# A ninth key block in 16-bit parts, halved products for a lone block, and re-placed tanh steps in a fused attention and MLP kernel

## The chip, the core and the metric

The kernel runs on one core of a Trainium2 chip. The metric is device time in microseconds for one launch; the table below has the median of three runs. The engines are named as in the profile: PE multiplies matrices (PEld is its weight load), DVE is the vector engine, ACT the scalar engine that evaluates exp and tanh, POOL the general engine, SP the engine that only issues DMAs.

## What is computed

The input `x` has 2048 tokens of 640 numbers. It is normalised once and goes into two branches whose results are added to `x`.

```python
xn = _layernorm(x, axis=-1)
# branch A: 32 heads of 20, softmax over 2048 keys
qkv = (xn @ wqkv) -> q, k, v
p = softmax(q @ k.T * 20 ** -0.5)
A = (p @ v) @ wo
# branch B: per token, 640 -> 1536 -> 640
y = _layernorm(xn, axis=-1)
B = gelu(y @ w1 + b1) @ w2 + b2
return x + A + B
```

All inputs and outputs are 32-bit floats, and the kernel keeps close to that precision: most products are made of two 16-bit parts of each factor, in three passes.

## The kernel before, in words

**Start and projections** (to about 215 us). `x` is normalised, transposed and multiplied by `wqkv` in four chunks of 512 tokens. At the very start PE has nothing to do until the first chunk is normalised; `warm(n)` (L231) fills such places with n multiplications of a constant tile. Between them `add_squares(i)` (L556) adds up the squares of the q weights, each waiting for a sum from ACT. Then four token blocks are transposed (L564 to L568), each after its normalisation on DVE (L270), and `scale_of` (L570) turns the sum of squares into the scale of the q weights. The projections `qkp` (L337) follow.

**Attention with the MLP in its gaps** (about 215 to 1271 us). The work is a list of 256 groups. A group is four blocks of 128 keys for one pair of heads and 512 tokens; four groups, key blocks 0 to 3, 4 to 7, 8 to 11 and 12 to 15, make a run over all keys, and there are 64 runs (16 head pairs, two halves of the tokens, two chunks in each half). For each key block `scores` (L742) makes the scores of two heads on PE (L748) and their exp on ACT (L750) into a 32-bit tile `p`. Three PSUM buffers hold scores.

`SPLIT` (L27) tells how a key block meets the values. For a **split** block `rest` (L757) subtracts on DVE the upper 16 bits of `p` (read as bf16, `upper`) from `p` itself and stores the rest as 16-bit `low` (L762); there are four buffers for `low`. `pv` (L767) then makes four products with the upper bits, two heads times the high and the low part of the values, and two with `low` and the high part of the values alone. For a **whole** block it makes two 32-bit products, one for each head. All of these are recorded at L779, in `product`. A product fills 32 of the 128 output rows: four products that go to the four different sets of 32 rows run side by side on PE, and each set of four is called a round here. With two split and two whole blocks in a group the upper bits take two rounds, the `low` products one, and the 32-bit products one, which PE runs as two matmuls each.

The order is written out by hand (L1191 to L1215). In a group come: the scores of two blocks; `tick()`, which lets each waiting side job emit its next step; the `low` of the first block; a piece of filling work on PE (`other`, L1177, which hands out 1.265 us for each group from a chain of MLP and projection work); the scores of the other two blocks; `tick()`; the `low` of the other blocks; and `pv` of the group **before**. DVE, ACT and PE each take their instructions in the order in which they were emitted.

The filling work is `layer1` (L1005: 30 matmuls `pu` for two of twelve blocks of the hidden layer, 256 tokens) and `layer2` (L1043: 36 matmuls `py`). Six `layer1` calls stand beside four `layer2` calls for the 256 tokens before: after the first and the fourth `layer1` no `layer2` follows, after the others one does (L1068 to L1075). For the first 256 tokens there is no `layer2` at all. All of these use one PSUM buffer, `m`, so the next call's first matmul waits until DVE has read the last one's result: `gelu` (L947) reads `pu` in its first step (L951), `addup` reads `py` (L981). `gelu` goes on in five more steps: two DVE operations on `u` and `w` (L953, L955), one more (L957), tanh on ACT (L961), and three on DVE (L963 to L965). If `reading[0]` is set, the tanh is put off by one `tick`, so that it does not stand in the half group in which ACT reads out the finished attention output (`ev`, L800). There is one buffer for `u` and one for `w`; when a new `gelu` begins, the one that is still active is run to its end first (L1020 to L1024).

**The end** (about 1271 us to the end). `projection` (L1112) makes the last product with `wo` (`z`, L1137) in 256-token pieces. For the tokens of the second half it needs the last heads' result, which `finish` (L861) divides by the softmax sums and writes to `oscr`; a piece reads it back as `ot` (L1087). `finish` waits a fixed number of ticks, `W1` before it adds the sums (L911, L913) and `W2` (L936) before it adds, multiplies and splits the result (L937 to L943).

Of the kernel before, what the change touches and what calls it, by code (L numbers as in the profile page):

```python
# [19 lines left out]
S, D, H, DH, F = 2048, 640, 32, 20, 1536  # L20
KD = D // P
KF = F // P
NKB = S // P
VW = DH + 1
PAD = 32 - VW
VROW = H * VW + PAD
SPLIT = (1, 1, 0, 0) * (NKB // 4)  # L27
NPAIR = H // 2
EPS = 1e-5
TOP = 15.5  # L30
# [14 lines left out]
def mha_mlp_kernel(tc, x, wqkv, wo, w1, b1, w2, b2, out):  # L45
    nc = tc.nc
# [3 lines left out]
    with (  # L50
# [23 lines left out]
        vhalf = vfull.bitcast(F16)  # L74
# [100 lines left out]
        with tc.tile_pool(name="pa", bufs=2) as pa, tc.tile_pool(name="pa1", bufs=1) as pa1, tc.manual_schedule():  # L175
# [55 lines left out]
            def warm(n):  # L231

                ps = psO.tile([P, 512], F32, tag="o", name="warm")
                for _ in range(n):
                    nc.tensor.matmul(ps[:, :P], ones, ones, start=True, stop=True)
# [322 lines left out]
                nc.tensor.matmul(pq[:, :1], ones, accs["q"][:, i : i + 1], start=i == 0, stop=i == KD - 1)  # L558

            add_squares(0)  # L560
            warm(3)
            add_squares(1)
            warm(4)
            for j in range(4):  # L564
                for k in range(KD - 1):
                    nc.tensor.transpose(pt[k][:, j * P : (j + 1) * P], xts[0][j][:, k * P : (k + 1) * P], ident)
# [101 lines left out]
        with ExitStack() as scope:  # L668
# [98 lines left out]
            def pv(units):  # L767

                g, hf, cc, kb0 = units[0][:4]
                if kb0 == 0:
                    pv.o = psO.tile([P, 512], F32, tag="o", name="o")
                    pv.begun = set()
                last = units[-1][3] == NKB - 1

                def product(q, src, v0, t):
                    nc.tensor.matmul(pv.o[32 * q : 32 * q + 32, :], src[:, v0 - PAD * (1 - q % 2) :][:, :32], t,  # L779
                                     start=q not in pv.begun, stop=last, skip_group_check=True)  # L780
                    pv.begun.add(q)

                split = [(u[3], upper(u[4]), u[5]) for u in units if SPLIT[u[3]]]
                whole = [(u[3], u[4]) for u in units if not SPLIT[u[3]]]
                of16 = lambda kb, a: 2 * PAD + kb * 2 * VROW + (2 * g + a) * 2 * VW
                of32 = lambda kb, a: PAD + kb * VROW + (2 * g + a) * VW
                for kb, up, _ in split:
                    for a in range(2):
                        product(2 * a, vhalf, of16(kb, a), up[:, a])
                        product(2 * a + 1, vhalf, of16(kb, a) + VW, up[:, a])  # L790
                for a in range(2):
                    for n, (kb, _, low) in enumerate(split):
                        product(2 * a + n % 2, vhalf, of16(kb, a), low[:, a])
                for a in range(2):
                    for n, (kb, pt) in enumerate(whole):
                        product(2 * a + n % 2, vfull, of32(kb, a), pt[:, a])
                if last:
                    if cc == 0:
                        evs[g, hf] = m1.tile([P, 2, 512], F32, tag="ev", name="ev")
                    nc.scalar.activation(evs[g, hf][:, cc], pv.o, AF.Copy)  # L800
                    if cc == 1:
                        unload(g, hf, evs.pop((g, hf)))
# [141 lines left out]
                    go(oscr[:, r0:r1, cols].rearrange("s d t -> d s t"), hl)  # L944
                ready[hf] += 1

            def gelu(ps, r2f, hT, f):  # L947
                u = m1.tile([P, 2, MC], F32, tag="u", name="u")
                w = m1.tile([P, 2, MC], F32, tag="w", name="w")
                scale_rows(r2f)  # L950
                nc.vector.tensor_mul(u, ps, r2f[:, None, :].to_broadcast([P, 2, MC]))  # L951
                yield 0.6
                nc.vector.tensor_add(u, u, b1t[:, f : f + 2, None].to_broadcast([P, 2, MC]))  # L953

                nc.vector.tensor_mul(w, u, u)  # L955
                yield 1.2
                nc.vector.scalar_tensor_tensor(w, w, 1.0 / 0.044715, u, ALU.add, ALU.mult)  # L957
                yield 0.6
                if reading[0]:
                    yield  # L960
                nc.scalar.activation(w, w, AF.Tanh, scale=0.7978845608028654 * 0.044715)  # L961
                yield
                nc.vector.scalar_tensor_tensor(u, w, 1.0, u, ALU.add, ALU.mult)  # L963
                nc.vector.tensor_scalar(hT[:, f : f + 2, 0, :], u, ch, None, ALU.mult)
                nc.vector.scalar_tensor_tensor(hT[:, f : f + 2, 1, :], u, ch, hT[:, f : f + 2, 0, :],  # L965
                                               ALU.mult, ALU.subtract)
                yield 1.7
# [37 lines left out]
            def layer1(mc, f):  # L1005
                xnt, r2f = xs[mc]
                if f == 0:
                    hTs[mc] = m0.tile([P, KF, 2, MC], F16, tag="hT", name="hT")
                ps = psM.tile([P, 2, MC], F32, tag="m", name="pu")
                for i in range(2):  # L1010
                    n = 0
                    fo_ = (f + i) % 4 * P
                    for k in range(KD):
                        for a, b in PASS:
                            nc.tensor.matmul(ps[:, i], w1v[:, k, (f + i) // 4, a, fo_ : fo_ + P], xnt[:, k, b, :],  # L1015
                                             start=(n == 0), stop=(n == 3 * KD - 1))
                            n += 1
                            if n % 3 == 0:
                                if i == 1 and n == 15:
                                    for it in [it for it in sides if it is active[0]]:  # L1020

                                        for _ in it:
                                            pass
                                        sides.remove(it)  # L1024
                                    active[0] = gelu(ps, r2f, hTs[mc], f)
                                    begin(active[0])
                                yield 0.3276
                if f == KF - 2:
# [75 lines left out]
                load_piece(0)  # L1104

            reading = [False]
            active = [None]
            done = [False]
            ended = [False]
            W1, W2 = 18, 5  # L1110

            def projection():  # L1112
                known = lambda c: split_done and ready[2 * c // NMC] == len(UNITS)
# [53 lines left out]
            with tc.manual_schedule():  # L1167
# [51 lines left out]
                n = 0  # L1219
# [27 lines left out]
def general(tc, nc, V, vscr, qkscr, oscr, accscr, gscale, ident, psS, psO, psM, project):  # L1247
# [2 lines left out]
    ds = bass.ds  # L1250
    nc.sync.dma_start(vscr, V)

    assert SPLIT == (1, 1, 0, 0) * (NKB // 4)
    with (
        tc.tile_pool(name="g2", bufs=2) as g2,
        tc.For_i(0, S, P) as t,
# [1 line left out]
        with tc.For_i(0, D, DH) as r:  # L1258
# [10 lines left out]
            for b in range(2):  # L1269
                nc.vector.tensor_add(vt[:, b::4, :], vp[:, b::4, :DH], vp[:, b::4, VW : VW + DH])  # L1270
# [63 lines left out]
```

## Time and profile before

| | us |
|---|---|
| median of 3 runs | 1337.33 (1336.65 to 1337.51) |
| the profiled execution, its own time | 1337.13 |
| span of its instructions | 1335.1 |
| ACT busy | 1128.6 |
| POOL busy | 37.5 |
| weight loads (PEld) busy, beside PE | 586.8 |

The time lies 2.03 us above the span of the same execution. Busy times are unions of instruction durations. Because matmuls are pipelined, the duration of one is longer than the distance between the starts of two; for what a matmul costs in a row of them, the distance between starts is to be read. A view in order of time gives in each line the start, the time from the first start to the last end, the engine, line, operation, tiles and shapes, how many instructions were merged (x8), and in brackets the idle time before them with what ended it.

### The profile page before, as it was taken

Reading aid. Unit: us, or ns where it says so; the run is one execution under the profiler, and the core shown is the slowest. Engines: PE = TensorE matmul, PEld = TensorE weight load, DVE = VectorE, ACT = ScalarE, POOL = GpSimd, SP = SyncE. Lnnn points to the kernel's source line nnn. Section 1 sums busy time; section 2 is a strip of 40 time slices with the busy share of each in tenths; the row PEclk is TensorE's granted clock in tenths of the full one; section 3 lists DMA queues with packets and bytes.
Section 4 is the critical chain, followed back from the end, with each engine's and each line's share of the span. In section 5 each row is a group of like instructions: output and inputs, shape, how many; then the busy total and the mean of one; then the engine's idle time right before and its main releaser. Section 6 shows DMA issues by size and latency. Waiting matters only on the chain.

```text
span 1335.1 us, 29057 instructions
## 1 busy us (share of the span) xinstructions
PE 1324.9 (99%) x11643; PEld 586.8 (44%) x11643; DVE 1055.2 (79%) x1428; ACT 1128.6 (85%) x1306; POOL 37.5 (3%) x86
## 2 busy tenths in 40 slices
PE   9999999999999999999999999999999999999998
PEld 6645546443434333434344344334433434333366
DVE  7756845998788888879887888888878888997732
ACT  7854425999999999999999999999999999999900
POOL 3010000000000000000000000000000000000000
PEclk9999999999999999999999999999999999999999
DMA  9869832111122323122422032323032323333376
GB/s 276 258 188 184 155 108 58 34 54 43 49 68 63 87 57 95 49 61 53 114 74 68 24 99 62 87 67 84 20 88 64 95 64 87 119 107 115 96 211 195
DMA packets 100150, 129.54 MB, mean 97 GB/s; under 512 B 24276, under 2 KB 66328, under 8 KB 100012
## 3 DMA queue, kind: packets, MB, share of 16 engines
q1 hardware_dynamic: 96652, 120.25, 32.3%
q0 software_dynamic: 2912, 6.90, 2.9%
q8 instruction: 92, 1.51, 0.5%
q10 hardware_dynamic: 448, 0.51, 0.1%
q14 instruction: 46, 0.38, 0.1%
HBM read 82.14 MB, written 42.51 MB: 93 GB/s over the span
## 4 chain that ended last, share of the span: by engine, by line
PE 86%; DVE 6%; DMA 5%; ACT 1%; issue 1%; SPq 0%; ACTq 0%; DVEq 0%
PE o L779 30%; PE s L748 19%; PE py L1051 13%; PE pu L1015 11%; PE qkp L337 5%; PE z L1137 4%; PE vp L410 3%; DVE low L762 2%; DMA xt<-in_A_x_dram 2%; DMA xnt<-row 1%; ACT p L750 1%; DMA qkscr<-qkhl 1%; DVE qkhl L353 1%; DVE st L255 0%; DMA w1t<-in_A_wqkv_dram 0%
## 5 line engine op out<-in xcount | busy, mean ns | idle before, releaser
L750 ACT ACTIVATE p<-s 128x1024 f32<-128x1024 f32 x1024 | 974.3, 1049 | 35.3 <-PE s L748 29.1
L762 DVE TENSOR_TENSOR low<-p 128x1024 f16<-128x1024 f32 x512 | 614.3, 1218 | 147.0 <-ACT p L750 145.9
L779 PE MATMUL o<-p,vfull 128*32 128x512 bf16 (+1 forms) x4096 | 429.4, 493 | 0.0
L748 PE MATMUL s<-qs,ks 61*128 61x512 f16 x2048 | 311.4, 381 | 0.2 <-ACT p L750 0.2
L748 PEld LDWEIGHTS <-ks 61*128 61x128 f16 x2048 | 61.2, 94 | 278.4 <-issue 276.8
L1051 PE MATMUL py<-w2t,hT 128*128 128x320 f16 x1152 | 178.5, 300 | 1.8 <-DVE u L951 1.8
L1015 PE MATMUL pu<-xm,w1t 128*128 128x256 f16 x1440 | 178.2, 273 | 0.1
L1015 PEld LDWEIGHTS <-w1t 128*128 128x128 f16 x1440 | 131.0, 98 | 63.9 <-issue 50.2
L1051 PEld LDWEIGHTS <-hT 128*128 128x128 f16 x1152 | 102.4, 98 | 89.8 <-issue 55.6
L337 PE MATMUL qkp<-xnt,wv 128*128 128x512 f16 x600 | 131.1, 379 | 0.0
L779 PEld LDWEIGHTS <-vfull 128*32 128x32 f16 x3072 | 59.9, 95 | 139.2 <-issue 108.0
L779 PE MATMUL o<-low,vfull 128*32 128x512 f16 x1024 | 102.1, 377 | 0.2
L337 PEld LDWEIGHTS <-wv 128*128 128x128 f16 x600 | 58.3, 98 | 69.5 <-DVE wv L451 1.0
L779 PEld LDWEIGHTS o<-p,vfull 128*32 128x32 f32 x2048 | 61.8, 108 | 53.1
L1137 PE MATMUL z<-w1t,ot 128*128 128x320 f16 x480 | 67.7, 299 | 0.7 <-DMA ot<-oscr 0.7
L410 PE MATMUL vp<-wv,xnt 128*128 128x320 f16 x480 | 66.9, 299 | 0.4 <-DVE qkhl L353 0.4
L352 ACT ACTIVATE qkhl<-qkp,qks 128x1024 f16<-128x1024 f32 (+1 forms) x24 | 23.2, 965 | 44.2 <-PE qkp L337 27.1
L1137 PEld LDWEIGHTS <-ot 128*128 128x128 f16 x480 | 45.8, 98 | 24.0 <-issue 5.5
L410 PEld LDWEIGHTS <-xnt 128*128 128x128 f16 x480 | 46.8, 98 | 19.0 <-issue 0.5
L1093 DVE SCALAR_TENSOR_TENSOR acc<-z,sc,acc 128x320 f32<-128x320 f32 x32 | 17.5, 549 | 40.1 <-PE z L1137 35.8
L353 DVE SCALAR_TENSOR_TENSOR qkhl<-qkp,qks,qkhl 128x1024 f16<-128x1024 f32 (+1 forms) x24 | 26.5, 1104 | 28.5 <-ACT qkhl L352 28.5
L800 ACT ACTIVATE ev<-o 128x512 f32<-128x512 f32 x64 | 39.5, 617 | 2.2 <-PE o L779 2.1
(191 smaller groups left out, 672.6 us busy)
## 6 DMA issues: line engine op xcount, KB each, us to landing
qkscr<-qkhl SPq DMA_DIRECT2D x40, 256.0 KB
opart<-ev SPq DMA_DIRECT2D x124, 80.0 KB
ks<-qkscr SPq DMA_DIRECT2D x120, 80.0 KB
qs<-qkscr SPq DMA_DIRECT2D x192, 40.0 KB
oa<-opart SPq DMA_DIRECT2D x32, 240.0 KB
xt<-in_A_x_dram SPq DMA_DIRECT2D x16, 320.0 KB
xscr<-xnt SPq DMA_DIRECT2D x4, 1280.0 KB
xm<-xscr SPq DMA_DIRECT2D x8, 640.0 KB
```

Of the source, the lines that this page charges most:

```text
L337: nc.tensor.matmul(ps[:, i, :], wv[:, k, q, a, mm * P : (mm + 1) * P], xnts[c][:, k, b, :], start=(k + n == 0), stop=(k == KD - 1 and n == 2))
L352: nc.scalar.activation(hl[:, 0, i0:i1], ps[:, i0:i1], AF.Copy, scale=a)
L353: nc.vector.scalar_tensor_tensor(hl[:, 1, i0:i1], ps[:, i0:i1], a, hl[:, 0, i0:i1], ALU.mult, ALU.subtract)
L410: nc.tensor.matmul(ps[:, hf, :320], xnts[c][:, k, a, j * P : (j + 1) * P], wv[:, k, 2, b, hf * 320 : (hf + 1) * 320], start=(n == 0), stop ...
L748: nc.tensor.matmul(ps[:, a, :], ks[64 * a : 64 * a + 61, kb * P : (kb + 1) * P], qs[64 * a : 64 * a + 61, cc * 512 : (cc + 1) * 512], star ...
L750: nc.scalar.activation(pt, ps, AF.Exp, scale=QS)
L762: nc.vector.tensor_sub(low, pt, upper(pt))
L779: nc.tensor.matmul(pv.o[32 * q : 32 * q + 32, :], src[:, v0 - PAD * (1 - q % 2) :][:, :32], t, start=q not in pv.begun, stop=last, skip_gr ...
L800: nc.scalar.activation(evs[g, hf][:, cc], pv.o, AF.Copy)
L1015: nc.tensor.matmul(ps[:, i], w1v[:, k, (f + i) // 4, a, fo_ : fo_ + P], xnt[:, k, b, :], start=(n == 0), stop=(n == 3 * KD - 1))
L1051: nc.tensor.matmul(ps[:, :320], hTs[mc][:, f, a, j * P : (j + 1) * P], w2v[:, f, b, hf * 320 : (hf + 1) * 320], start=(n == 0), stop=(n == ...
L1137: nc.tensor.matmul(ps[:, :320], ot[:, k, a, j * P : (j + 1) * P], wov[:, k, b, h * 320 : (h + 1) * 320], start=(n == 0), stop=(n == 3 * KD ...
```

## The change

It has five parts.

1. `SPLIT` gets a ninth block: key block 6 is split too, so the second group of each run has three split blocks and one whole one. DVE subtracts 64 more `low` tiles in all, and one more value block is split in the projections (L422).
2. In `pv` a lone block, the third `low` of such a group and its one whole block, has its 512 tokens halved: one half goes to one set of 32 output rows and the other half to the other set, which are added in the end as before. The third `low` block is then four products of 256 tokens, and the whole block four 32-bit products of 256 tokens.
3. `gelu` gets an argument `room`: the tanh is put off only where it is set, for calls other than those of the first 256 tokens and other than the first and fourth of six. The forced end of an active `gelu` goes.
4. `warm(3)` and `warm(4)` at the start become `warm(2)` and `warm(1)`.
5. `W1, W2` become 17 and 3.

```diff
-SPLIT = (1, 1, 0, 0) * (NKB // 4)
+SPLIT = (1, 1, 0, 0, 1, 1, 1, 0) + (1, 1, 0, 0) * 2
...
             add_squares(0)
-            warm(3)
+            warm(2)
             add_squares(1)
-            warm(4)
+            warm(1)
...
-                def product(q, src, v0, t):
-                    nc.tensor.matmul(pv.o[32 * q : 32 * q + 32, :], src[:, v0 - PAD * (1 - q % 2) :][:, :32], t,
-                                     start=q not in pv.begun, stop=last, skip_group_check=True)
+                def product(q, src, v0, t, c0=0, c1=512):
+                    nc.tensor.matmul(pv.o[32 * q : 32 * q + 32, c0:c1], src[:, v0 - PAD * (1 - q % 2) :][:, :32],
+                                     t[:, c0:c1], start=q not in pv.begun, stop=last, skip_group_check=True)
                     pv.begun.add(q)
+
+                def whole_tokens(a, n, alone, src, v0, t):
+
+                    if alone:
+                        product(2 * a, src, v0, t, 0, 256)
+                        product(2 * a + 1, src, v0, t, 256, 512)
+                    else:
+                        product(2 * a + n % 2, src, v0, t)
...
-                for a in range(2):
-                    for n, (kb, _, low) in enumerate(split):
-                        product(2 * a + n % 2, vhalf, of16(kb, a), low[:, a])
+                for n0 in range(0, len(split), 2):
+                    for a in range(2):
+                        for n, (kb, _, low) in enumerate(split[n0 : n0 + 2]):
+                            whole_tokens(a, n, n0 + 1 == len(split), vhalf, of16(kb, a), low[:, a])
                 for a in range(2):
                     for n, (kb, pt) in enumerate(whole):
-                        product(2 * a + n % 2, vfull, of32(kb, a), pt[:, a])
+                        whole_tokens(a, n, len(whole) == 1, vfull, of32(kb, a), pt[:, a])
...
-            def gelu(ps, r2f, hT, f):
+            def gelu(ps, r2f, hT, f, room):
+
...
-                if reading[0]:
+                if room and reading[0]:
                     yield
...
                                 if i == 1 and n == 15:
-                                    for it in [it for it in sides if it is active[0]]:
-
-                                        for _ in it:
-                                            pass
-                                        sides.remove(it)
-                                    active[0] = gelu(ps, r2f, hTs[mc], f)
-                                    begin(active[0])
+                                    begin(gelu(ps, r2f, hTs[mc], f, mc > 0 and f // 2 % 3 > 0))
...
-            W1, W2 = 18, 5
+            W1, W2 = 17, 3
```

In the order of the built program PE's instructions other than those of `pv` stand as before, but for the four warm products less and for the softmax-sum product of the end (L929), which moves ahead of three `z` matmuls. Six of the 48 tanhs move ahead of three exps, and the three DVE operations behind each of them ahead of one `low`. In the end part DVE's last two steps of `finish` (L941, L943) move ahead of one `acc` operation (L1093). On SP the issues that change places are stack, part-sum and MLP loads that swap with their neighbours. On POOL one more memset stands at the start. The code after the `If` (`general`) does not run for these inputs; it is adapted to the new `SPLIT`.

More of the change, by code (lines that the diff above doesn't have):

```diff
@@ L1106, in mha_mlp_kernel @@
             reading = [False]
-            active = [None]
             done = [False]
             ended = [False]
-            W1, W2 = 18, 5
+            W1, W2 = 17, 3
             def projection():
@@ L1251, in general @@
     nc.sync.dma_start(vscr, V)
-    assert SPLIT == (1, 1, 0, 0) * (NKB // 4)
+    assert SPLIT == tuple(int(i % 4 < 2 or i == 6) for i in range(NKB))
     with (
@@ L1268, in general @@
             vp = vr.bitcast(F16)
-            for b in range(2):
-                nc.vector.tensor_add(vt[:, b::4, :], vp[:, b::4, :DH], vp[:, b::4, VW : VW + DH])
+            for b in (slice(0, None, 4), slice(1, None, 4), slice(6, 7)):
+                nc.vector.tensor_add(vt[:, b, :], vp[:, b, :DH], vp[:, b, VW : VW + DH])
             sf = g2.tile([P, S], F32, tag="sf", name="sf")
```

## The prediction

> **What bounds the kernel now.** I read the page first, then the stages by window, then one group in order of time, then the list of waits.
>
> ```profile
> span 1335.1 us, 29057 instructions
> PE 1324.9 (99%) x11643; PEld 586.8 (44%) x11643; DVE 1055.2 (79%) x1428; ACT 1128.6 (85%) x1306; POOL 37.5 (3%) x86
> PE 86%; DVE 6%; DMA 5%; ACT 1%; issue 1%; SPq 0%; ACTq 0%; DVEq 0%
> ```
>
> The last line is from the chain that ended last: PE has 86% of it. Whether PE is really dense is seen in one group (start, duration, engine):
>
> ```profile
> 521.24 0.61 PE L748 MATMUL s<-qs,ks 61*128 61x512 f16 x4
> 521.78 0.64 PE L779 MATMUL o<-p,vfull 128*32 128x512 bf16 x8
> 522.24 0.40 PE L779 MATMUL o<-low,vfull 128*32 128x512 f16 x4
> 522.46 1.04 PE L779 MATMUL o<-p,vfull 128*32 128x512 f32 x8
> 523.43 0.61 PE L748 MATMUL s<-qs,ks 61*128 61x512 f16 x4
> ...
> 526.38 2.35 DVE L762 TENSOR_TENSOR low<-p 128x1024 f16<-128x1024 f32 x2
> ...
> 529.09 2.36 DVE L762 TENSOR_TENSOR low<-p 128x1024 f16<-128x1024 f32 x2 [0.36 <-ACT p L750]
> ...
> 530.34 0.39 PE L779 MATMUL o<-low,vfull 128*32 128x512 f16 x4
> ```
>
> From start to start, the two upper-bit rounds take 0.46 us (0.23 a round), the `low` round 0.22, the 32-bit round 0.97. Every group of the attention stage shows these distances to a hundredth or two, but for some twenty places that add up to about 6 us. So PE is the bound there, and what is taken off PE comes off the time, as long as the others keep up:
>
> ```profile
> 225.00:250.00 25.00, 25.00 (x239) 11.00 (x235) 24.31 (x31) 23.89 (x28) 0.00 (x0) 1.00 0.01 1
> 250.00:300.00 50.00, 49.76 (x483) 21.22 (x479) 48.47 (x58) 49.01 (x57) 0.90 (x1) 1.00 0.20 58
> ...
> 1100.00:1200.00 100.00, 100.00 (x927) 39.44 (x925) 90.77 (x126) 96.27 (x107) 1.70 (x2) 1.00 0.35 100
> 215.00:1272.00 1057.00, 1054.73 (x9862) 424.00 (x9861) 894.79 (x1066) 1016.11 (x1137) 15.01 (x18) 1.00 0.26 72
> ```
>
> The columns after the length are busy PE, PEld, DVE, ACT, POOL. Over the whole stage DVE is busy 85%, ACT 96%; from 225 to 300 us, where the filling is `layer1` alone, DVE has 72.78 of 75 us, and from 1100 to 1200 us 91%.
>
> **The change part by part, against the profiled execution's 1337.13 us** (0.2 us below the median shown, 2.03 above its span).
>
> *The ninth block on PE.* A second group has one more upper-bit round (+0.23), a `low` round of half length (+0.11) and a halved 32-bit round. Of that round's 0.97 I take 0.86, four times the 16-bit round, for the streaming of 512 tokens (an estimate); half of it goes (-0.43), the rest stays. Sum -0.10, in 64 groups **-6.5 us**. If all of the 0.97 halves it is -9; if the short rounds gain only half as much beyond the streaming, -3. Can four products with four weight loads start in 0.11 us? The nearest row has 16 products of 128 tokens into the same four sets of rows, each with its own weights:
>
> ```profile
> 41.74 0.41 PE L382 MATMUL norms<-sq,heads 128*32 128x128 bf16 x16
> ...
> L382 PE MATMUL norms<-sq,heads 128*32 128x128 bf16 x160 | 3.7, 221 | 0.0
> ```
>
> 0.41 us from first start to last end, less the 0.22 of one, is 0.19 for three rounds, 0.06 each. So 0.11 is enough. The Trainium skill, "TensorE: Matmul & The Clock Gate", section Back-to-back issue gap, says the opposite: a stream of weight loads and matmuls is given there with about 81 ns a pair at 128 columns, whatever the matmul alone would need. By that rule (an estimate) four pairs would take 0.32 us, a halved round would gain nothing over the 0.22 of a full one, and this sum would be a loss; the L382 row, at 0.015 us a pair, disagrees.
>
> *The ninth block on DVE.* 64 subtractions more. Two in a row take 2.35 and one 1.22, so each costs 1.13 us in a busy queue: 72 us on 895, or 92% of a stage some 7 us shorter. They stand behind the `low` of block 5 and in front of everything DVE does in the next half group, among it the `low` of blocks 8 and 9 and, after the first of these, the reading of the `m` buffer. The third subtraction also gets a new wait: with four buffers it takes the one that the group before has in use until its `low` round on PE, in the same half group. In the rows above that round is over at 530.73 while DVE's own second subtraction lasts until 531.45: I cost this wait at nothing; if DVE runs ahead it can be a few tenths, which DVE then has to spare.
>
> Where DVE is full, the cost is direct. A group lasts 4.09 us, from
>
> ```profile
> L762 DVE TENSOR_TENSOR low<-p x512: 1152/1218/1227, 219.9 to 1267.6; 128x1024 f16<-128x1024 f32 x171
>   ACT p L750: 145.9, 123
> ```
>
> (1047.7 over 256). From 225 to 300 us there are 75/16.4 = 4.6 second groups: 5.2 us more of DVE, 0.5 us less of PE time, and 2.2 us idle to take it: **+3.5 us**.
>
> Elsewhere it is a question of slack. The second row above says that DVE waited for an exp 123 times, 1.2 us each: a gap that can swallow one subtraction comes every 8.5 us on average, and the last product of a third group is used some 6 us after the inserted work, so in about half of the cases no gap comes in between. Then it matters how early the `low` was. Reading all 256 `low` rounds in order of time against the end of their second subtraction, the middle one had 1.9 us, a quarter had under 1.2, and a few none at all:
>
> ```profile
> 623.31 1.22 DVE L762 TENSOR_TENSOR low<-p 128x1024 f16<-128x1024 f32 x1
> 624.44 0.68 DVE L963 SCALAR_TENSOR_TENSOR u<-w,u 128x512 f32<-128x512 f32 x1
> ...
> 625.69 0.75 DVE L965 SCALAR_TENSOR_TENSOR hT<-u,sc,hT 128x512 f16<-128x512 f32 x1
> 626.36 1.22 DVE L762 TENSOR_TENSOR low<-p 128x1024 f16<-128x1024 f32 x1
> 627.49 0.68 DVE L939 TENSOR_TENSOR oa<-oa,rb 120x512 f32<-120x512 f32 x1
> 628.09 1.22 DVE L762 TENSOR_TENSOR low<-p 128x1024 f16<-128x1024 f32 x1
> ...
> 629.20 0.55 PE L779 MATMUL o<-low,vfull 128*32 128x512 f16 x4
> ```
>
> Here a second group's last `low` is the one at 623.31, DVE has no gap from there to 629.31, and the third group's round at 629.20 already waited for it. The inserted 1.13 us falls in whole on PE. Outside 225 to 300 us there are 59 second groups. Third groups' rounds: half without a gap, a third of those short by 0.6 on average, 59/6 x 0.6 = 6. Their own rounds: the half round is used 0.43 later than the full one, so 0.7 of slack is needed; an eighth had less, 0.4 on average, 3. The `m` buffer, read in about 20 third groups, a third of them with under 1.1 to spare: 6 x 0.5 = 3, less what PE's earlier stalls give back, 2. Together **+11 us**, between 4 (gaps take nearly all) and 18 (as crowded as from 225 to 300).
>
> *The tanh.* The six that move are those where DVE stood waiting for a put-off tanh and the next reading of `m` was queued behind it. Twice PE waited:
>
> ```profile
> 488.17 0.64 ACT L961 ACTIVATE w<-w 128x512 f32<-128x512 f32 x1
> 488.85 0.69 DVE L963 SCALAR_TENSOR_TENSOR u<-w,u 128x512 f32<-128x512 f32 x1 [0.20 <-ACT w L961]
> 490.20 0.60 PE L748 MATMUL s<-qs,ks 61*128 61x512 f16 x4
> 490.95 0.69 DVE L951 TENSOR_TENSOR u<-pu,r2f 128x512 f32<-128x512 f32 x1
> 491.70 1.25 PE L1051 MATMUL py<-w2t,hT 128*128 128x320 f16 x8 [0.90 <-DVE u L951]
> ...
> PE py L1051 <- DVE u L951: 1.8, 2, 0.9
> ```
>
> The scores at 490.20 take 1.50 us to the next start instead of 0.54; with the `low` round behind, 1.15 us in each of the two places: **-2.3 us** (0 if the ninth block fills the gap again, -3 with the smaller waits).
>
> *Start and end.* Transposes can follow the normalised blocks, which come every 0.55 us:
>
> ```profile
> 10.55 2.18 DVE L270 TENSOR_SCALAR xt<-xt,mv,r 128x640 f32<-128x640 f32 x4
> 10.77 1.16 PE L235 MATMUL warm<-ones 128*128 128x128 f32 x8
> 11.77 0.60 PE L566 MATMUL pt<-ident,xt 128*128 128x128 f32 x4
> 13.40 0.63 PE L566 MATMUL pt<-ident,xt 128*128 128x128 f32 x4
> ```
>
> Six of the eight matmuls between go; the first block is ready at 11.10 and the last at 12.73, where its transposes now start at 13.40: **-0.6 us**. At the end PE waits 0.7 us for `ot`, which hangs on `finish`; one 0.5 us step of DVE leaves that chain:
>
> ```profile
> 1287.37 0.54 DVE L1093 SCALAR_TENSOR_TENSOR acc<-z,sc,acc 128x320 f32<-128x320 f32 x1
> 1297.79 25.98 PE L1137 MATMUL z<-w1t,ot 128*128 128x320 f16 x190 [0.70 <-DMA ot<-oscr]
> ```
>
> **-0.5 us**, bounds 0 and -1. The extra memset and the ninth value block's split fall where POOL and DVE are idle half the time: 0.
>
> *Sum:* 1337.1 - 6.5 + 3.5 + 11 - 2.3 - 0.6 - 0.5 = **1341.7 us**.
>
> **The rivals.**
>
> *DVE keeps up (faster).* For it: 160 us idle in the stage against 72 added, and the middle `low` is 1.9 us early, more than one subtraction. Against it: the first stage is full. If the gaps take all but 3.5 to 5 us, the time is 1337.1 - 9.9 + 4 = 1331; it is under 1334.5 as long as all stalls together stay below 7.3 us.
>
> *Gain and stalls cancel.* Stalls of 7.3 to 12.6 us in all give 1334.5 to 1339.8, middle 1337. This case also holds the one where ACT is the bound and PE's gain is lost: for it stands ACT's 1016 of 1057 us, against it the 41 us left, and PE's steady distances. The Trainium skill, "Perfetto Trace Analysis", section Identifying the Most-Contended Engine, takes occupancy as the measure for the scalar engine and not for PE, which would name ACT here; by that, -6.5 would be 0.
>
> *The halved rounds are no shorter.* Then a second group is 0.23 + 0.22 longer, +29 us: 1377. Against it speaks L382.
>
> **How the numbers follow.** DVE late, as summed: 0.52, likeliest, by itself 1339.8 to 1349. DVE keeps up: 0.27. Cancelled: 0.18. No shorter rounds: 0.03. About 0.2% (2.7 us) is what a measurement of this kernel tells from no change: faster 0.27, same 0.18, slower 0.55. The range reaches down to 1330 (stalls of only 3 us; a tenth lies below) and up to 1349 (stalls of 22 us, the upper bounds of both stall terms; under a tenth above).
>
> **What would show it.** Right: DVE near 99% busy from 225 to 300 us and over 91% in the stage; PE waiting before `low` rounds of second and third groups and before `pu` and `py`, 14 us together; the 490 and 1000 us waits smaller; 0.1 us less from the upper-bit round to the next scores in second groups. Wrong: PE as dense as before (the first rival), or 32-bit rounds of 0.97 us in second groups (the last).

## The result and the profile after

The kernel after takes **1350.35 us** (median of 6 executions, 1347.42 to 1356.07), the kernel before 1336.63 beside it (1335.90 to 1337.51): ratio 1.0104, 95% interval 1.009 to 1.0118. It is 13.7 us slower, where 4.6 were forecast. The profiled execution took 1348.59 us. Its page:

```profile
span 1346.4 us, 30230 instructions
...
PE 1327.7 (99%) x12147; PEld 601.5 (45%) x12147; DVE 1126.8 (84%) x1493; ACT 1131.6 (84%) x1306; POOL 37.8 (3%) x87
...
PE 68%; DVE 17%; DMA 6%; ACT 4%; issue 4%; SPq 1%; POOL 0%; DVEq 0%; ACTq 0%
```

PE is "busy" 99% as before, because the ends of its matmuls are modelled; it is the chain that ended last that tells the change: PE has 68% of it, not 86%, and DVE 17%, not 6%. The view in order of time shows gain and loss side by side (start, duration, engine):

```profile
627.81 2.35 DVE L762 TENSOR_TENSOR low<-p 128x1024 f16<-128x1024 f32 x2
...
629.34 0.87 PE L779 MATMUL o<-p,vfull 128*32 128x512 bf16 x12
630.03 0.50 PE L779 MATMUL o<-low,vfull 128*32 128x512 f16 x8
630.08 0.68 DVE L973 SCALAR_TENSOR_TENSOR u<-w,u 128x512 f32<-128x512 f32 x1
...
630.35 0.61 PE L779 MATMUL o<-p,vfull 128*32 128x256 f32 x8
630.80 0.49 DVE L974 TENSOR_SCALAR hT<-u,sc 128x512 f16<-128x512 f32 x1
...
630.89 0.61 PE L748 MATMUL s<-qs,ks 61*128 61x512 f16 x4
631.32 0.75 DVE L975 SCALAR_TENSOR_TENSOR hT<-u,sc,hT 128x512 f16<-128x512 f32 x1
...
631.99 1.22 DVE L762 TENSOR_TENSOR low<-p 128x1024 f16<-128x1024 f32 x1
...
633.13 0.68 DVE L948 TENSOR_TENSOR oa<-oa,rb 120x512 f32<-120x512 f32 x1
...
633.62 0.38 PE L779 MATMUL o<-low,vfull 128*32 128x512 f16 x1
633.73 1.22 DVE L762 TENSOR_TENSOR low<-p 128x1024 f16<-128x1024 f32 x1
...
635.00 0.40 PE L779 MATMUL o<-low,vfull 128*32 128x512 f16 x3 [1.00 <-DVE low L762]
```

From start to start the second group's products take 0.69 (upper bits), 0.32 (`low`) and 0.54 us (halved 32-bit round): 1.55 us instead of 0.46 + 0.22 + 0.97 = 1.65. That is the gain, 0.1 us a group. The two subtractions at 627.81 are blocks 5 and 6. From there DVE has no gap until block 9's `low` is done at 634.95, and three of the four products of the third group's `low` round, which began at 633.62, start only at 635.00. This is the place and the order of events that the forecast drew.

Stage by stage (columns as in the prediction: PE, PEld, DVE, ACT, POOL), and the waits (total us, times, longest):

```profile
225.00:250.00 25.00, 23.72 (x247) 10.63 (x236) 24.55 (x31) 23.45 (x28) 0.00 (x0) 1.00 0.01 1
250.00:300.00 50.00, 48.62 (x485) 21.27 (x486) 49.33 (x58) 46.98 (x55) 0.00 (x0) 1.00 0.20 56
...
1100.00:1200.00 100.00, 98.41 (x959) 39.54 (x958) 94.05 (x124) 95.84 (x108) 1.70 (x2) 1.00 0.33 99
215.00:1284.00 1069.00, 1058.36 (x10385) 439.59 (x10384) 965.33 (x1130) 1019.28 (x1138) 15.01 (x18) 1.00 0.26 72
```

```profile
DVE low L762 <- ACT p L750: 89.1, 96, 8.2
...
PE o L779 <- DVE low L762: 4.2, 7, 1.0
...
DVE low L762 <- PE o L779: 2.4, 3, 1.3
...
PE pu L1025 <- DVE u L961: 1.9, 4, 0.8
PE py L1055 <- DVE xb L991: 1.7, 2, 1.1
```

DVE is full from 225 to 300 us (73.88 of 75) and at 90% over the stage; the gaps in which it waits for an exp fell from 145.9 us to 89.1. The list of waits counts only time in which no matmul runs. Read start to start against each product's usual distance, PE loses 22.3 us in the stage (6.0 before), 16.4 more (before rounding), and its dense rest is 5.8 us shorter: 16.4 - 5.8 = 10.6, the growth from first to last scores (1048.3 to 1058.8). "Lost" below is always this reading.

The other 3 us of the 13.7 can't be read from one execution: the kernel after spreads over 8.7 us, the kernel before over 1.6.

### The profile page after: what moved, and what is told of

It is laid out like the page before. It is cut to its first block, busy times and chain, and to the rows that moved or that the text cites. A ratio compares the mean times of both kernels' runs of the same rounds, so it can differ in the third digit from the quotient of the medians.

```text
span 1346.4 us, 30230 instructions
## 1 busy us (share of the span) xinstructions
PE 1327.7 (99%) x12147; PEld 601.5 (45%) x12147; DVE 1126.8 (84%) x1493; ACT 1131.6 (84%) x1306; POOL 37.8 (3%) x87
## 4 chain that ended last, share of the span: by engine, by line
PE 68%; DVE 17%; DMA 6%; ACT 4%; issue 4%; SPq 1%; POOL 0%; DVEq 0%; ACTq 0%
PE o L779 23%; PE s L748 14%; PE py L1055 10%; DVE low L762 8%; PE pu L1025 8%; PE qkp L337 5%; PE z L1140 5%; ACT p L750 3%; PE vp L410 3%; DMA xt<-in_A_x_dram 2%; DVE u L961 1%; DMA wos<-in_A_wo_dram 1%; DVE u L963 1%; DVE u L973 1%; DVE hT L974 1%
## 5 line engine op out<-in xcount | busy, mean ns | idle before, releaser
L762 DVE TENSOR_TENSOR low<-p 128x1024 f16<-128x1024 f32 x576 | 686.3, 1219 | 92.6 <-ACT p L750 89.1
L779 PE MATMUL o<-p,vfull 128*32 128x512 bf16 (+2 forms) x4352 | 420.2, 462 | 0.0
L779 PEld LDWEIGHTS <-vfull 128*32 128x32 f16 x3584 | 76.7, 95 | 170.7 <-issue 124.3
L779 PE MATMUL o<-low,vfull 128*32 128x512 f16 (+1 forms) x1280 | 116.9, 357 | 5.3 <-DVE low L762 4.2
L352 ACT ACTIVATE qkhl<-qkp,qks 128x1024 f16<-128x1024 f32 (+1 forms) x24 | 23.2, 965 | 45.6 <-PE qkp L337 29.1
L353 DVE SCALAR_TENSOR_TENSOR qkhl<-qkp,qks,qkhl 128x1024 f16<-128x1024 f32 (+1 forms) x24 | 26.5, 1105 | 28.6 <-ACT qkhl L352 28.5
```

What stands on the lines that cost most here:

```text
L352: nc.scalar.activation(hl[:, 0, i0:i1], ps[:, i0:i1], AF.Copy, scale=a)
L353: nc.vector.scalar_tensor_tensor(hl[:, 1, i0:i1], ps[:, i0:i1], a, hl[:, 0, i0:i1], ALU.mult, ALU.subtract)
L762: nc.vector.tensor_sub(low, pt, upper(pt))
L779: nc.tensor.matmul(pv.o[32 * q : 32 * q + 32, c0:c1], src[:, v0 - PAD * (1 - q % 2) :][:, :32], t[:, c0:c1], start=q not in pv.begun, stop ...
```

## The experiments

Each ran beside the kernel before, on the same chip (median 1336.55 to 1337.08 over four such sets). "Old cover" means `warm(3)` and `warm(4)`.

### The parts apart

**Parts 1 and 2 alone** (the kernel after with parts 3, 4 and 5 undone).

> The kernel after with parts 3 to 5 undone: ninth block and halved rounds alone. Theory (the forecast's sum, with its stall terms as the trace after shows them): -6.2 on PE, about +16 of waits behind a late DVE, so 1346 to 1350; and the waits on DVE before the 32-bit, pu and py products stand in its trace as in that of the kernel after. Rival (the loss comes from the moved tanhs, which now stand in half groups that read out ev, or from the end part): 1333 to 1340 here.

1352.40 us, ratio 1.012 (1.0105 to 1.0134), all within 1.7 us.

```profile
PE o L779 <- DVE low L762: 4.9, 8, 1.0
PE py L1060 <- DVE u L960: 3.5, 5, 0.9
PE pu L1024 <- DVE u L960: 2.3, 4, 0.8
PE py L1060 <- DVE xb L990: 1.7, 2, 1.1
```

The theory's cause holds, but the time lies 2.4 us above its upper end (1350), and the loss is larger than in the kernel after: PE loses 27.4 us, **21.4 more than before**, of which 14.8 at `low` products and the rounds behind them and 6.5 before `pu` and `py`. Less 5.7 of gain on PE that is +15.7, and +15.8 was measured.

**Parts 3 to 5 alone** (before, eight split blocks).

> The kernel before with parts 3 to 5 alone, eight split blocks. Forecast's terms: tanh -2.3, start -0.6, end -0.5, so 1333.2; the first scores at about 217.6 us instead of 218.2, no wait of PE over 0.5 us near 490 and 1000 us, and 68.2 us from the last scores to the end of the span instead of 68.7. Rival (start and end are set by DMAs or by something other than the steps that move; only the tanh counts): 1334.3. Rival (the three steps cost as much as they bring, and the kernel after lost its -3.4 here): 1336 to 1339.

1335.27 us, but from 1333.95 to 1342.66; ratio 0.9997 (0.9986 to 1.0009). None of the three expectations fits: six executions lie at 1334 to 1335.3, five from 1337 up. Something in these parts makes the time unsteady, so they were taken apart.

**Part 3 alone, the tanhs.**

> The kernel before with the moved tanhs alone (part 3). Forecast's term: -2.3, so 1334.3; by the distance from first to last scores in the trace of parts 3 to 5 alone (1047.0 against 1048.3) -1.3, so 1335.3. In either case the times spread over 2 us, as those of the kernel before do.

1335.26 us within 1.7 us; ratio 0.9988 (0.998 to 0.9997). It is the smaller figure. The waits before `py` are gone, but a new one stands before the scores, since each moved tanh now runs ahead of three exps:

```profile
PE s L748 <- ACT p L750: 1.2, 4, 0.4
```

**Parts 3 and 5** (before with `W1, W2 = 17, 3` too).

> The kernel before with the moved tanhs and W1, W2 = 17, 3 (parts 3 and 5). The tanhs alone gave 1335.26, 1.4 us less than before. Forecast's term for the end: another -0.5, so 1334.8, with less than 0.7 us of waiting for ot before the z products. Rival (the last transfer of ot sets the end, whatever DVE does ahead of it): 1335.3 and the same wait.

1334.58 us (1334.06 to 1337.87), ratio 0.9987 (0.9978 to 0.9996). The median is 0.7 us below that of the tanhs alone, but the two are not told apart: the intervals overlap, and five of the eleven executions lie above 1335.3, under the old cover. The profiled one (1337.41) is of these. In it the write to `oscr` is issued 0.33 us earlier after the last scores (23.04 against 23.37), but the wait it was to shorten is longer, 1.74 us instead of 0.70:

```profile
1298.08 25.98 PE L1131 MATMUL z<-w1t,ot 128*128 128x320 f16 x190 [1.74 <-DMA ot<-oscr]
```

So the profile does not show the forecast gain at the end; the landing of `ot` decided in this execution. This is the fastest version of all that compute the whole.

**Part 4 alone, the cover.**

> The kernel before with warm(2) and warm(1) in place of warm(3) and warm(4), nothing else. Forecast's term: -0.6, so 1336.0, with a spread of about 2 us as the kernel before has. Theory from the trace of the parts 3 to 5 alone, whose granted clock is 0.50 from 11.0 to 14.2 us: the shorter cover brings PE under a level of activity at which its clock is halved for 3.4 us, in some executions; then the median is 1336 to 1339 and the times spread over 4 us or more. Rival (that drop was chance or belongs to the other edits): spread of 2 us.

1336.39 us, from 1335.64 to 1341.09: seven of twelve at 1335.6 to 1336.5 (the forecast gain of some 0.5), one at 1337.7 and four at 1339.9 to 1341.1. The spread that the theory named came. The profiled execution has the halved clock (0.50 from 11.0 to 14.4 us), but it is the one at 1337.7, not one of the four.

**The kernel after with the old cover.**

> The kernel after with warm(3) and warm(4) as before. If the shorter cover at the start is what spreads the times of the kernel after (1347.4 to 1356.1): 1348 to 1350 within 2 us, 0 to 2 us below the median of after. If the spread comes from the late DVE: the same spread as after, 1350.

1347.13 us **within 1.1 us**, ratio 1.0078 (1.0065 to 1.0091). Its trace has the waits of the kernel after (22.2 us lost). The time is 0.9 us below the lower end expected. So 3.2 us of the median, and most of the spread, go with the shorter cover. Not every late execution does: parts 3 and 5 above spread over 3.8 us under the old one.

### Is it DVE?

**No third subtraction, the products kept.**

```diff
+                if kb == 6:
+                    unit.append(None)
+                elif SPLIT[kb]:
...
+                split = [(kb, up, low or split[1][2]) for kb, up, low in split]
```

> The kernel after, whose block 6 gets no subtraction: its low product takes the low of block 5 (wrong low bits for block 6, all else the same). PE does every product of the kernel after, DVE has the work of the kernel before. Theory (all of the added waits are DVE's 1.13 us): the added waits go, 1336.6 - 6.2 - up to 3.4 = 1327 to 1331, stage near 1042 us. Rival (the waits come from PE's changed order, from the halved rounds or from ACT being full): 1340 or more, with waits of PE that no DVE ends.

1330.75 us (1329.06 to 1337.08), ratio 0.9962 (0.995 to 0.9974). And the same under the old cover:

> The kernel after with the old cover at the start and no subtraction for block 6 (its low product takes the low of block 5, so block 6's low bits are wrong). With the shorter cover this was 1330.75, from 1329.06 to 1337.08. If the shorter cover makes the late executions: 1329 to 1331, within 2 us. If the lighter DVE or the ninth block does: the same spread of 8 us.

**1330.13 us**, 1329.64 to 1330.67, ratio 0.995 (0.9937 to 0.9962). PE loses 4.7 us, little more than with the tanhs alone (4.0). Every product of the kernel after runs here, so the products and their order cost nothing; what is lost is lost to 64 subtractions.

**The subtraction without the products** (before, one more).

```diff
+                if kb == 6:
+                    idle = ptp.tile([P, 2, 512], F16, tag="low", name="idle", bufs=GRP)
+                    nc.vector.tensor_sub(idle, pt, upper(pt))
```

> The kernel before with one more subtraction for key block 6, at the place of the change and in the same four buffers, its result read by nobody; PE's products are those before. Theory: DVE's cost alone. The forecast's terms give +14.5 (1351); by the stalls of the trace after +16 (1353), a few us less where a group that is 0.1 us longer gives DVE room. Rival (DVE has the room, the waits are due to the changed products): 1336 to 1340.

1354.41 us, ratio 1.0129 (1.0115 to 1.0144): +17.8 for 64 results that nobody reads, more than either figure expected; the rival is out. PE loses 17.3 us more than before in the stage:

```profile
PE py L1054 <- DVE u L954: 3.7, 5, 0.9
PE o L782 <- DVE low L765: 2.9, 4, 0.9
PE pu L1018 <- DVE u L954: 2.7, 4, 1.0
```

**Half a subtraction.**

```diff
+                    n = 1 if kb == 6 else 2
+                    nc.vector.tensor_sub(low[:, :n], pt[:, :n], upper(pt)[:, :n])
```

> The kernel after with the old cover at the start (1347.13), block 6's subtraction made for one of its two heads alone: 128x512 instead of 128x1024, some 0.6 us instead of 1.13. The other head's low product takes the low of block 5 (wrong low bits for half of block 6, all else the same). PE's products are unchanged. Waits in proportion to DVE's load: half way between no third subtraction and a whole one, 1338 to 1339. Waits that grow faster than the load (gaps of 0.4 to 0.6 us a group take most of the short one): 1333 to 1336. Slower than that (what counts is that anything stands there): 1341 or more.

1335.42 us, ratio 0.9991 (0.9982 to 1.0). The groups of DVE by form, then the stage:

```profile
L763 DVE TENSOR_TENSOR low<-p 128x512 f16<-128x512 f32 x64 | 43.8, 685 | 0.0
```

```profile
215.00:1272.00 1057.00, 1052.77 (x10387) 438.25 (x10385) 933.01 (x1130) 1016.02 (x1138) 15.00 (x18) 1.00 0.26 72
```

| third subtraction | DVE busy in the stage, us | lost on PE, us | time, us |
|---|---|---|---|
| none | 894.8 of 1050 (85%) | 4.7 | 1330.13 |
| half | 933.0 of 1057 (88%) | 10.0 | 1335.42 |
| whole | 965.0 of 1067 (90%) | 22.2 | 1347.13 |

The first half adds 38.2 us of DVE work and costs 5.3 us, the second adds 32.0 and costs 11.7. The waits grow faster than the load, as the middle theory said, though the halved version lies at its upper end. Why they do is not shown. A longer subtraction outruns the slack of more rounds, and one subtraction may use up gaps that the next would have needed; the runs change the length of the subtraction and not their number, so they don't separate the two.

### The place of the subtraction

**A group earlier** (block 2 as the ninth, `SPLIT = (1, 1, 1, 0) + (1, 1, 0, 0) * 3`).

> The kernel after with the old cover at the start (1347.13) and key block 2 instead of block 6 as the ninth: the third subtraction stands one group earlier in each run of four. In the trace of before DVE's gaps in the four groups are 0.39, 0.58, 0.41 and 0.39 us on average; an inserted subtraction then meets the largest first. Theory (DVE's gaps nearby decide how much of the subtraction is swallowed): 2 to 6 us less, 1341 to 1345, with less waiting of PE before low products. Rival (only DVE's load in all counts, wherever it stands): 1346 to 1348.5.

1344.98 us, ratio 1.0062 (1.0048 to 1.0075), 2.2 below 1347.13, and 19.5 us lost instead of 22.2. The place counts, by the smallest amount that the theory allowed; most of the loss stays.

**Half a group later.**

```diff
+                            if kb0 == 8:
+                                rest(prev[2])
                             rest(units[0])
...
-                                rest(u)
+                                if u[3] != 6:
+                                    rest(u)
```

> The kernel after with the old cover at the start (1347.13); the third subtraction of a second group is emitted half a group later, behind the side jobs' next steps and ahead of the subtraction of block 8. It is needed at the end of that group still. Theory (a third of the added waits come from DVE's steps queued behind the third subtraction, the reading of the m buffer above all): the waits before pu and py fall from 5.4 to some 2 us and the time to 1342 to 1345; the waits before the halved low products grow a little. Rival (DVE's load in all decides): 1346 to 1349.

1361.70 us, ratio 1.0184 (1.017 to 1.0198): 14.6 more, a miss for both theories.

```profile
PE o L779 <- DVE low L762: 20.6, 23, 1.7
```

The waits before `pu` and `py` did fall, from 5.4 to 3.1 us, but the halved `low` round now waits: 26.5 us lost in front of the halved products where it was 4.1. Behind the side jobs the third `low` is simply too late for its own use.

**On POOL.** `(nc.gpsimd if kb == 6 else nc.vector).tensor_sub(low, pt, upper(pt))`

> The kernel after with the third subtraction of the second group on POOL instead of DVE; PE's products are all those of the kernel after. Its duration on POOL stands in no trace here. If it stays under some 4 us (the result is needed a group later) and leaves DVE's own durations alone, DVE's load is that of before and the time that of the kernel without the third subtraction: 1329 to 1332. If POOL takes longer, or slows DVE while both run: PE waits before the halved low rounds, 1340 or more. The start has the shorter cover, so a few executions may be 4 us longer.

1407.05 us, ratio 1.0528 (1.0515 to 1.0542). The duration itself was no bar (min, median, max in ns):

```profile
L762 POOL TENSOR_TENSOR low<-p x64: 1892/2190/5311, 224.4 to 1327.4; 128x1024 f16<-128x1024 f32 x64
```

Three other things were. POOL also issues the load that adds `b2` to `xb`, which waits for an earlier transfer, and the subtraction stands behind it:

```profile
892.75 0.87 POOL L1045 DMA_DIRECT2D xb<-in_B_b_dram  x1 [26.14 <-DMA qs<-qkscr]
893.36 2.19 POOL L762 TENSOR_TENSOR low<-p 128x1024 f16<-128x1024 f32 x1
895.61 0.40 PE L779 MATMUL o<-low,vfull 128*32 128x256 f16 x4 [10.37 <-POOL low L762]
```

```profile
PE o L779 <- POOL low L762: 29.1, 8, 10.4
PE o L779 <- DVE low L762: 11.0, 25, 0.8
```

Of the eight waits for POOL, 29.1 us in all, the five longest stand behind such a load. The long stalls also cost PE its clock: in the profiled execution five stretches of the stage, 27.3 us together, ran at 0.50 (third figure from the end), which is up to 13.7 us of the loss:

```profile
889.20:899.40 10.20, 3.79 (x24) 1.70 (x24) 0.90 (x1) 1.94 (x2) 2.80 (x2) 0.50 0.46 112
```

And a DVE subtraction that starts while POOL's runs is held up, so DVE's own waits did not go either:

```profile
527.61 2.58 POOL L762 TENSOR_TENSOR low<-p 128x1024 f16<-128x1024 f32 x1 [15.29 <-ACT p L750]
...
529.62 1.65 DVE L762 TENSOR_TENSOR low<-p 128x1024 f16<-128x1024 f32 x1 [1.18 <-ACT p L750]
```

### The cover at the start

**No cover at all** (before without the two calls).

> The kernel before without the two warm calls between the sums of the start (warm(3) and warm(4) become nothing). With warm(2) and warm(1) four of twelve executions took 3 to 5 us more. Theory (the cover at the start is what keeps the executions together): more of them are late, half or most, and the median is 1338 to 1341; the profile, if of a late one, shows whether the time goes in the first 20 us, or later in the projections as in the one late execution profiled so far (a wait of 3.8 us near 156 us and a halved clock behind it). Rival (the late ones of the shorter cover were chance): 1335.5 to 1336.5, within 2 us.

1340.33 us, from 1335.84 to 1347.66, ratio 1.0029 (1.0016 to 1.0042): eleven of twelve above 1338.9. With the seven filler products of `warm(3)` and `warm(4)` one of 23 executions of the kernel before, beside them, did so; with three, four of twelve; with none, eleven of twelve. The profiled one took 1345.27 us. Its windows, and those of the kernel before (PE first, the granted clock third from the end):

```profile
8.00:11.00 3.00, 1.59 (x12) 1.23 (x10) 2.17 (x9) 2.30 (x6) 1.80 (x2) 1.00 1.03 398
11.00:12.00 1.00, 0.72 (x7) 0.75 (x8) 1.00 (x3) 0.97 (x4) 0.00 (x0) 0.96 1.04 410
12.00:15.00 3.00, 3.00 (x17) 3.00 (x16) 0.70 (x2) 1.40 (x5) 0.00 (x0) 0.50 1.06 292
...
155.00:160.00 5.00, 2.79 (x22) 2.03 (x21) 4.64 (x7) 5.00 (x9) 0.00 (x0) 1.00 0.58 163
160.00:165.00 5.00, 2.94 (x12) 1.68 (x12) 4.93 (x8) 1.31 (x2) 0.00 (x0) 0.71 0.90 219
```

```profile
8.00:11.00 3.00, 2.20 (x19) 2.00 (x19) 2.78 (x10) 2.29 (x6) 1.80 (x2) 1.00 1.02 404
11.00:12.00 1.00, 1.00 (x11) 1.00 (x11) 1.00 (x3) 0.97 (x4) 0.00 (x0) 1.00 1.05 410
12.00:15.00 3.00, 2.75 (x27) 2.66 (x26) 1.44 (x7) 1.62 (x6) 0.00 (x0) 1.00 1.05 291
...
155.00:160.00 5.00, 4.62 (x49) 3.21 (x52) 4.79 (x14) 2.04 (x4) 0.00 (x0) 1.00 1.12 268
```

The longest gap of PE in the first of these stretches without the cover is this:

```profile
9.55 0.38 PE L558 MATMUL mxq<-acc,ones 128*128 128x1 f32 x2 [0.72 <-ACT junk L546]
```

PE, busy for 1.59 of the 3 us from 8 to 11, gets half its clock from 11.9 to 15.3 us, so the transposes run at half speed and `qkp` starts at 16.57 instead of 15.51. Later, near 157 us, it waits again:

```profile
162.06 4.15 PE L410 MATMUL vp<-wv,xnt 128*128 128x320 f16 x17 [4.27 <-DVE qkhl L353]
```

That wait was 0.38 us before; there ACT stands until a store of `qkhl` has landed (5.72 us, 3.87 before), and the clock drops a second time. The first scores start at 226.3 instead of 218.2 us. The profiles of parts 3 to 5 and of part 4 alone show the first drop too (clock 0.50 from 10.9 to 14.3 and from 11.0 to 14.4 us), without a second one; that of the kernel without the third subtraction under the new cover shows the second wait (3.83 us) and a drop behind it without the first drop.

Two things are to be kept apart here. A drop takes at most 1.7 us of PE's time (half of 3.4), and `qkp` started 1.1 us later with it. The executions that are over 5 us late and were profiled (no cover, and the kernel without the third subtraction at 1335.88) have the long wait near 157 us, one of them without the first drop. Waits of 1.2 to 2.2 us stand in the same place under the old cover, in the profiles of the dead copy, of the half subtraction and of the third `low` half a group later. That the cover changes how many executions are late is shown by the counts; why the store is late in some was not settled.

Whether the short cover costs PE its first drop differs between executions, and the profiles show with what. In parts 3 to 5 and in part 4 alone PE was fast early (20 matmuls from 5.05 to 7.00 us): its first fillers were done at 8.3 and 8.4 us, it waited 1.2 and 1.4 us for ACT's first sum, and the drop followed. In the kernel after and in the one without the third subtraction it got through 12 matmuls in the same time, the fillers lasted until 9.8 us, the wait was 0.34 us or none, and no drop came. The stretch in which the two differ, parts 3 to 5 first, then the kernel after:

```profile
7.50:9.50 2.00, 0.84 (x8) 0.65 (x6) 1.55 (x6) 0.80 (x3) 1.69 (x3) 1.00 1.03 388
```

```profile
7.50:9.50 2.00, 2.00 (x20) 2.00 (x20) 1.86 (x7) 0.20 (x1) 1.69 (x4) 1.00 1.04 401
```

**A longer first cover** (`warm(33)` for `warm(25)`, then two and one).

> The kernel before with warm(2) and warm(1) and with the first warm(25) made warm(33): the eight matmuls go into the time in which PE waits for ACT's first sum, from about 8.8 to 9.6 us, and the transposes are as early as with the shorter cover. Theory (the halved clock from 11 to 14 us follows too little activity of PE in the 3.4 us before): all executions near 1336.2, within 2 us, as the lower two thirds of those with the shorter cover alone. Rival (it hangs on what runs after 9.6 us, or on the transfers): some executions at 1340 to 1341 again.

1338.26 us, from 1337.49 to 1338.74 but for one of 1340.76; ratio 1.0008 (0.9999 to 1.0017). Half right: no drop stands in the profile, PE has no gap before its first sum there, `qkp` starts at 15.24 us, and ten of eleven executions are within 1.3 us; but the median is 2 us above the forecast. In the profiled one (1338.25) the wait for `ot` at the end is 1.3 us longer than in the kernel before (1.98 instead of 0.70), which the edit doesn't touch; it stays open.

## Why the prediction failed

The direction was right, the time 8.7 us too low and outside the range. Two terms of the sum failed: DVE late, forecast at +14.5 us, cost 21.4, and the start, forecast at -0.6, cost 3.2. The tanhs and the end brought 2.5 us more than forecast and hid part of that. What the forecast named as signs came, one of them a little short: DVE 98.5% busy from 225 to 300 us, 90% over the stage where over 91 was named, PE late before `low`, `pu` and `py` (16.4 us more than before in the kernel after, where 14 was named), 0.1 us less a group. By its own steps:

| step | forecast, us | measured, us | from |
|---|---|---|---|
| base | 1337.1 | 1336.6 | medians |
| ninth block on PE | -6.5 | -5.7 | dense part of the stage, parts 1 and 2 alone |
| DVE late | +3.5 + 11 | +21.4 | lost on PE, parts 1 and 2 alone |
| tanh and end | -2.3 - 0.5 | -5.3 | 1352.40 to 1347.13 |
| start | -0.6 | +3.2 | 1347.13 to 1350.35 |
| sum | 1341.7 | 1350.2 (median 1350.35) | |

- **The ninth block on PE** was right, halved rounds and all: the four 256-token products add 0.10 us to the `low` round (0.32 after 0.22), as L382 had promised, and the rival with no shorter rounds is out.
- **DVE late** is the step that failed first: the mechanism was right (no third subtraction, no loss), the size was not. From 225 to 300 us 3.5 were forecast and 4.8 are lost in parts 1 and 2 alone; elsewhere 11 (at most 18) against 16.6. The forecast set each subtraction against the slack that the trace of before showed, as if it came alone, and that price came out a third too low. The three sizes of the subtraction show that the price bends: the second half of it costs twice the first. Put by place, the `m` buffer was furthest off: 3 were forecast for it outside the first 75 us, 2 after what earlier stalls give back, and 6.5 are lost before `pu` and `py` in the whole stage. What in the estimate of slack was wrong, its sampling or the treatment of each subtraction by itself, stays open.
- **The tanh** alone brought -1.4, not -2.3, since its move puts a wait of its own before the scores. Together with the ninth block it was worth more: of the waits before `pu` and `py`, 3.9 us went. The forecast had the opposite as its bound ("0 if the ninth block fills the gap again"). The share of the end edit in the -5.3 was not measured by itself.
- **The end**: no run has part 5 by itself. With the tanhs it is 0.7 us lower in the median, within the scatter, and its profile has a longer wait for `ot`; so -0.5 is neither shown nor refuted.
- **The start** is the step that put the time out of the range; the 1347.13 us with the old cover lie within it. The forecast counted the eight matmuls as time in front of the transposes only, which the better executions of part 4 alone bear out (-0.5), and never asked what they covered. With the shorter cover more executions are late, by PE's halved clock, by the long wait near 157 us or by both; how the cover leads to the second is open. The Trainium skill, "TensorE: Matmul & The Clock Gate", section What's actually happening, has this rule: a halved clock after an idle window of about 3.4 us, on a window that runs free. The 3.4 us that the drop lasts agree, and so does the free run: without the cover the clock rises at 5.10 us and drops at 11.92 and 162.11 us, which is 2 and 46 times 3.413 us later. But no gap of PE between 8 and 12 us is longer than 0.72 us there. Nor does the share of busy time decide: PE was busy for 1.71 us of the 3.4 before that first drop, and in parts 3 and 5 this stretch, as thin and also one such window, cost it nothing:

```profile
1295.40:1298.80 3.40, 1.66 (x13) 0.98 (x12) 0.55 (x1) 0.00 (x0) 0.00 (x0) 1.00 0.81 211
```

  What of PE's work keeps the clock up is not shown by these runs.
- The new wait of the third subtraction for a `low` buffer, put at nothing, came 3 times in 64 groups (2.4 us of DVE's time): small.
- **The rivals.** "DVE keeps up" is what the kernel without the third subtraction does (1330.1 against 1331 forecast for it). ACT is not the bound: the same ACT work fits into 1330.

The fastest version that computes the whole is the kernel before with the moved tanhs and new `W1, W2`: 0.9987 of before (0.9978 to 0.9996). No version with a ninth block computed in full beat the kernel before.

## What to carry to other kernels

A second engine at 85% is not 15% free: here the first 38 us of work added to it cost 5.3 us, and the next 32 cost 11.7. The price of an insertion is better measured by a dead copy of it, with nothing else changed: +17.8 us here against +14.5 on paper, and 21.4 lost in parts 1 and 2. Small fillers ahead of the first real work may do more than fill; before they are taken out, ask what they cover. And a median of few executions hides a start that goes one of two ways: look at the spread first.

## What was not expected of the hardware

- TensorE's granted clock went to 0.50 for 3.4 us after 3 us in which PE was busy for 1.59, with no gap above 0.72 us; with 2.20 of 3 us busy in the same place it stayed at 1.00. Later in a kernel it also stayed at 1.00 over 3.4 us with 1.66 busy.
- Twelve or twenty matmuls in the same 1.95 us of the start: when the clock first rises differs between executions, and a fixed number of fillers covers a different time.
- A 128x1024 subtraction to 16 bits takes POOL 2.19 us (median), DVE 1.22. The two mostly take turns. In the rows above POOL's ends at 530.19; DVE's, begun at 529.62, takes 1.65 us, the 0.57 left of POOL's and 1.08 of its own. So it was for 25 of the 29 DVE subtractions that began while one of POOL ran; the other four kept their 1.22 us beside subtractions of POOL that took 3.6 to 5.3. The Trainium skill, "GPSIMD Engine Reference", section 1. Specifications, names a shared SBUF interface with contention for DVE instructions with two SBUF inputs, and the trace agrees.
